# Attention and two-layer FFN on one core: the low part of the weights by an accumulating on-chip transfer, and longer planned TensorE steps for batch 0

## The chip, the cores and the metric

The kernel runs on one core of one Trainium2 chip. The metric is the device time of one execution in microseconds (us), the median of several runs. A profile of one further execution gives the rows that are read below. Engines are named as in the profile: PE (TensorE matrix multiply), PEld (its weight loads), DVE (VectorE), ACT (ScalarE), POOL (GpSimd), SP (SyncE, which issues most transfers).

## What is computed

For each of 8 batches and 8 heads, 576 tokens of 64 numbers: a softmax attention over means of 4 tokens (144 by 144, repeated back to 576) plus a softmax attention over a band of 7 tokens. The sum, 4608 tokens of 512 numbers, goes through a two-layer network:

```
x = attn_out.transpose(0, 2, 1, 3).reshape(B * S, H * D)     # 4608 x 512
h = x @ w_in                                                 # 512 x 2048
g = h * np.cos(h)
return g @ w_out                                             # 2048 x 512
```

The inputs are float32 and the weights arrive as float64. Every product is made of three reduced-precision ones (high by high, high by low, low by high), so each weight, each x and each g is split into a high part, rounded to the matrix format, and a low part, the value minus its high part.

## The kernel before, in words

The network is cut into 12 tiles of 384 tokens and 16 chunks of 128 hidden columns. For each tile and chunk, `gemm1` (L688) makes 12 products of 384 columns, a chain of ACT and DVE steps forms the function (L697 to L706), and `gemm2` (L724) makes 9 products of 512 columns. The first three tiles, which are batches 0 and 1, go through the chunks in groups of four; from tile 3 on each tile takes all 16 chunks at once. Only the first 48 of 192 steps therefore meet a chunk of weights for the first time.

Attention goes by units: a batch and a pair of heads. `u_qk` loads q and k and sums groups of four (L480 on DVE, or L473 and L475 on POOL), `u_v` loads and sums v (L494, L495), `u_s` makes the scores on PE (`l_mm` L518, local; `d_mm` L526, pooled) and the softmax on DVE, ACT and POOL (L537 to L589), `u_t` turns the pooled probabilities (L609) and copies them out (L455, L456), and `u_pv` multiplies with v (L626 pooled, L637 local), adds both (L645) and splits the result into the x tiles (L660 high, L389 low).

Each of the 32 blocks of weights (w_in and w_out, 16 chunks) is loaded by SP (L400) as words and split by `w_split`. ACT takes the absolute value of the upper word into a scratch slot v (L410), DVE builds the float32 value there in four instructions (L411, L413, L415, L417), ACT or DVE writes the high part (L421 or L422), and `sub` writes the low part, v minus high: one tensor_tensor at L389 on POOL, or on DVE where the planner prefers it. v is one of three slots cut from the buffer that later holds the high part of x tile 3.

The order on every engine is that of a planner (`Plan.schedule`). Each step gets an engine, a planned duration, the steps it depends on and sometimes a latency `lat`. The planner runs a list schedule forward and backward eight times, picks an engine where a step has alternatives, and the instructions are issued in the order of the planned starts, so every engine works in order through that list. After planning, a loop puts matmuls on the identity matrix (L841), whose result is never used, into the planned gaps of PE before 300 us. Before each of batch 0's scores, turns and products it puts at least two of them (`warm=2`):

```
n = int((o.start - s[0] - CFG["fgap"]) / (0.43 if ahead or last < 60 else 0.3)) if s else 0
for _ in range(max(n, CFG["warm"] if ahead else 0)):
```

Late partial outputs of tiles 0 to 2 are already written by accumulating transfers that POOL issues (L749, planned at 1.0 us on POOL and a latency of 2.5 us).

Of the kernel before, what the change touches and what calls it, by code (L numbers as in the profile page):

```python
# [12 lines left out]
F32 = mybir.dt.float32  # L13
# [3 lines left out]
AF = mybir.ActivationFunctionType  # L17
ALU = mybir.AluOpType
# [268 lines left out]
def _act(n, psum=True, extra=0):  # L287
    return n * 0.000833 + (0.051 if psum else 0.093) + 0.093 * extra
# [11 lines left out]
def attn_ffn_kernel(ctx: ExitStack, tc: tile.TileContext, qT, kT, vdn, vl, w_in, w_out, out):  # L300
    nc = tc.nc
    pe, act, dve, pool, sp = nc.tensor, nc.scalar, nc.vector, nc.gpsimd, nc.sync
# [6 lines left out]
    pl = Plan()  # L309
# [5 lines left out]
    def psum(tag):  # L315
        pl.banks.append((tag, pl.buf(lambda: ps.tile([P, 512], F32, name="bank", tag=tag, bufs=1), tag)))
        return pl.banks[-1][1]
# [69 lines left out]
    def sub(n, out, in0, in1, **kw):  # L387

        f = lambda e: lambda: e.tensor_tensor(out=out(), in0=in0(), in1=in1(), op=ALU.subtract)  # L389
        pl.op("POOL", _pool(n), f(pool), alts=[("DVE", _dve(n), f(dve))], shares=True, **kw)  # L390
# [11 lines left out]
    def w_split(k, c):  # L402

        pl.name = "w_split"
        wd_b, w = words[(k, c)], wgt[(k, c)]
        wd, n = wd_b.get, DM
        nstage[0] += 1
        v = cut(xx[0], DM * (nstage[0] % 3), [P, DM])
        vi = lambda: v.get().bitcast(I32)
        pl.op("ACT", _act(n, False), lambda: act.activation(v.get(), wd().bitcast(F32)[:, :, 1], AF.Abs), r=[wd_b], w=[v], shares=True)  # L410
        pl.op("DVE", 0.5, lambda: dve.tensor_scalar(out=v.get(), in0=v.get(), scalar1=2.0 ** -15, scalar2=F64_TOP,  # L411
                                                    op0=ALU.max, op1=ALU.min), w=[v], shares=True)
        pl.op("DVE", 0.5, lambda: dve.tensor_scalar(out=vi(), in0=vi(), scalar1=3, scalar2=0x3FFFFFF8,  # L413
                                                            op0=ALU.logical_shift_left, op1=ALU.bitwise_and), w=[v], shares=True)
        pl.op("DVE", 0.7, lambda: dve.scalar_tensor_tensor(out=vi(), in0=wd()[:, :, 1], scalar=-0x40000000, in1=vi(),  # L415
                                                               op0=ALU.bitwise_and, op1=ALU.bitwise_or), r=[wd_b], w=[v], shares=True)
        pl.op("DVE", 0.7, lambda: dve.scalar_tensor_tensor(out=vi(), in0=wd()[:, :, 0], scalar=29, in1=vi(),  # L417
                                                               op0=ALU.logical_shift_right, op1=ALU.bitwise_or), r=[wd_b], w=[v], shares=True)
        h = pl.buf(None)
        hi = lambda: w.get()[:, 0]  # L420
        pl.op("ACT", _act(n, False), lambda: act.activation(hi(), v.get(), AF.Copy), r=[v], w=[h], pw=[w],  # L421
              alts=[("DVE", _dve(n / 2), lambda: dve.tensor_copy(hi(), v.get()))])  # L422
        sub(n, lambda: w.get()[:, 1], v.get, lambda: hi().bitcast(F32), r=[v, h], pw=[w])


    st = {}
# [3 lines left out]
                k=([P, SP_], 1, 1, 0), ptd=([HD, 2, 2, SD], 1, 1, 0),  # L430
# [16 lines left out]
    def bank(b, kind):  # L447

        if b == 0:
            tags = ("pa.0", "po.0", "pa.1", "po.1") if kind == "s" else ("ph.0", "ph.1", "pa.2")  # L450
            return psum(tags[int(pl.turn("early" + str(kind == "s"), len(tags))[-1])])
        return psum(pl.turn("pa", 3))

    def evac(n, dst, src, bk, t, scale=1.0):
        pl.op("ACT", _act(n), lambda: act.activation(dst(), src(), AF.Copy, scale=scale), r=[bk], pw=[t],  # L455
# [44 lines left out]
    def u_s(b, pr):  # L500
        pl.name = "u_s"
        u = st[(b, pr)]
        q, k, qkd = u["q"], u["k"], u["qkd"]
        sml, smd = ub(b, pr, "sml"), ub(b, pr, "smd")
        banks = [bank(b, "s") for _ in range(2)]
        loc, poo = [pl.buf(None) for _ in banks], [pl.buf(None) for _ in banks]

# [4 lines left out]
        def l_mm():  # L512

            for n in range(2 * NSEG):
                for h in range(2):
                    for e in range(2):
                        hs, o, c = slice(64 * h, 64 * h + 64), (8 * (n // 4) + 4 * e + n % 4) * BQ, LQ + BS * (n % NSEG)
                        pe.matmul(banks[n // NSEG].get()[64 * h + BS * e:64 * h + BS * (e + 1), c:c + BS],  # L518
                                  q.get()[hs, o:o + BS], k.get()[hs, o:o + BS], start=True, stop=True)
        pl.op("PE", 0.95, l_mm, r=[q, k], pw=banks, w=loc)  # L520

        def d_mm():
            for i in range(2):
                for h in range(2):
                    hs = slice(64 * h, 64 * h + 64)
                    pe.matmul(banks[h].get()[:HD, i * SD:(i + 1) * SD], qkd.get()[hs, 0, i * HD:(i + 1) * HD], qkd.get()[hs, 1, :],  # L526
                              start=True, stop=True)
        pl.op("PE", 0.65, d_mm, r=[qkd], pw=banks, w=poo)


        mxl, su = sb("mxl", 2, [P, 2 * NSEG]), sb("su", 2, [P, 2 * NSEG + 4])
# [8 lines left out]
        n = 2 * NSEG * BS  # L540
# [7 lines left out]
        for h in range(2):  # L548
# [3 lines left out]
            if not early:  # L552
                using(banks[h], pl.op("DVE", _dve(2 * SD), lambda h=h: dve.tensor_tensor(
                    out=smd.get()[:, h], in0=dq(h), in1=mxd.get()[:, h].unsqueeze(2).broadcast_to([HD, 2, SD]), op=ALU.subtract),
                    r=[poo[h], mx], pw=[smd]))
# [38 lines left out]
    def u_t(b, pr):  # L594
        pl.name = "u_t"
        u = st[(b, pr)]
        sml, smd = u["sml"], u["smd"]
        ptl, ptd = ub(b, pr, "ptl"), ub(b, pr, "ptd")

        pl.op("DVE", _dve(2 * NSEG * BS), lambda: dve.transpose(ptl.get().rearrange("p s q -> p (s q)"),  # L600
                                                                sml.get().rearrange("p s n -> p (s n)")), r=[sml], w=[ptl])
        for h in range(2):
            bk = bank(b, "t")

            def t_mm(h=h, bk=bk):
                for kh in range(2):
                    for qh in range(2):
                        o = kh * SD + qh * HD
                        pe.transpose(bk.get()[:HD, o:o + HD], smd.get()[:, h, qh, kh * HD:(kh + 1) * HD], ident[:HD, :HD])  # L609
            pl.op("PE", 4 * 0.061, t_mm, r=[smd], w=[bk])  # L610
            evac(2 * SD, lambda h=h: ptd.get()[:, h],
                 lambda bk=bk: bk.get()[:HD, :2 * SD].rearrange("p (a n) -> p a n", a=2), bk, ptd)
        u["ptl"], u["ptd"] = ptl, ptd

    def u_pv(b, pr):
        pl.name = "u_pv"
        u = st.pop((b, pr))
        ptl, ptd, vd, vt = (u[n] for n in ("ptl", "ptd", "vd", "vl"))
        xd, xs = ub(b, pr, "xd"), ub(b, pr, "xs")
        banks = [bank(b, "v") for _ in range(2)]  # L620
        poo, loc = pl.buf(None), [pl.buf(None) for _ in banks]

        def d_mm():
            for kh in range(2):
                for h in range(2):
                    pe.matmul(banks[0].get()[64 * h:64 * h + 64, 2 * SD:3 * SD], vd.get()[:, kh, 64 * h:64 * h + 64],  # L626
                              ptd.get()[:, h, kh, :], start=(kh == 0), stop=(kh == 1))
        pl.op("PE", 0.64, d_mm, r=[vd, ptd], pw=[banks[0]], w=[poo])

        def l_mm():  # L630
            for a in range(NSEG // 2):
                for i in range(4):
                    for e in range(2):
                        for h in range(2):
                            r = slice(64 * h + 32 * e, 64 * h + 32 * e + 32)
                            o = (4 * a + i) * BQ
                            pe.matmul(banks[e].get()[64 * h:64 * h + 64, o:o + BQ], vt.get()[r, a, i, :], ptl.get()[r, 4 * a + i, :BQ],  # L637
                                      start=True, stop=True)
        pl.op("PE", 1.52, l_mm, r=[vt, ptl], pw=banks, w=loc)

        evac(SD, xd.get, lambda: banks[0].get()[:, 2 * SD:3 * SD], banks[0], xd, scale=0.25)
        xd.w[-1].deps += poo.w
        half = [pl.buf(None) for _ in range(2)]
        for e in range(2):
            pl.op("DVE", _dve(S // 2), lambda e=e: dve.tensor_tensor(  # L645
                out=xs.get().rearrange("p (a e n r) -> p a e n r", e=2, a=NSEG // 2, r=4)[:, :, e],
                in0=banks[e].get()[:, :12 * BQ].rearrange("p (a n r) -> p a n r", a=NSEG // 2, r=4),
                in1=xd.get().rearrange("p (a e n) -> p a e n", e=2, a=NSEG // 2)[:, :, e].unsqueeze(3).broadcast_to(
                    [P, NSEG // 2, BQ, 4]), op=ALU.add), r=[banks[e], loc[e], xd], pw=[xs], w=[half[e]])
        lo = 0  # L650
        while lo < S:

            tt = tile_of(b * S + lo)
            to = min(S, FROM[tt] + SIZE[tt] - b * S)
            a, m = b * S + lo - FROM[tt], to - lo
            written[tt] += m
            done = pl.buf(None)
            hi = lambda tt=tt, a=a, m=m: x_tile(tt)[0][:, pr, a:a + m]
            src = lambda lo=lo, to=to: xs.get()[:, lo:to]
            pl.op("ACT", _act(m, False), lambda hi=hi, src=src: act.activation(hi(), src(), AF.Copy),  # L660
                  r=[xs], w=[done], pw=[x_b[tt]], alts=[("DVE", _dve(m / 2), lambda hi=hi, src=src: dve.tensor_copy(hi(), src()))])
            sub(m, lambda tt=tt, a=a, m=m: x_tile(tt)[1][:, pr, a:a + m], src, lambda hi=hi: hi().bitcast(F32),
                r=[xs, done], pw=[x_b[tt]])
            lo = to
# [108 lines left out]
    for c in range(NC):  # L773
        for k, d in (("i", 0.0), ("o", 0.7)):
            t = need[c]
# [103 lines left out]
```

## Time and profile before

| | |
|---|---|
| median of 3 runs | 1028.74 us (1027.08 to 1028.91) |
| profiled execution, its own time | 1031.63 us |
| its span, first to last instruction | 1029.5 us |
| busy in the span | PE 97%, PEld 84%, DVE 66%, ACT 59%, POOL 22% |
| mean granted PE clock | 0.983 of full speed |

The span is what the trace covers; the execution's own time has 2.1 us around it. Busy shares are averages over a start, in which attention of the first two batches and the first weights are prepared, and a long stretch of matrix products. The matmuls at L841 count as busy too.

### The profile page before, as it was taken

The numbers are of one execution on the slowest core, as the hardware profiler recorded it, in microseconds if no ns is written. First come the engines' busy times: TensorE is split into PE (matmuls) and PEld (weight loads), VectorE is DVE, ScalarE is ACT, GpSimd is POOL, SyncE is SP. The second block draws the span as 40 slices with busy tenths as digits, with TensorE's granted clock in tenths as the row PEclk, the third lists the DMA queues.
The fourth block names the chain that finished last, engine by engine and source line by source line (L and its number), as shares of the span: only waits on it lengthen the run. The fifth ranks groups of instructions, "written<-read, shape, count | busy, mean of one in ns | idle before, by whom it ended". The sixth has DMA issues, their size and how long they took to land.

```text
span 1029.5 us, 25935 instructions
## 1 busy us (share of the span) xinstructions
PE 1003.0 (97%) x11068; PEld 864.9 (84%) x11068; DVE 676.9 (66%) x1353; ACT 610.6 (59%) x1176; POOL 228.8 (22%) x274
## 2 busy tenths in 40 slices
PE   7889999999999999999999999999999999999998
PEld 4557788889988888889898888888888888899997
DVE  6699889996478668564738856755646865543443
ACT  2546577786566666565646655655655765655554
POOL 5596424433135201010103300101002410000000
PEclk8988899999999999999999999999999999999999
DMA  9762751434245312100202401200101310000000
GB/s 265 237 221 85 242 183 46 61 59 62 32 106 144 76 50 75 59 25 28 76 6 76 133 28 38 96 25 28 55 27 43 120 51 1 32 1 1 31 1 31
DMA packets 36450, 76.11 MB, mean 74 GB/s; under 512 B 3440, under 2 KB 11632, under 8 KB 36336
## 3 DMA queue, kind: packets, MB, share of 16 engines
q1 hardware_dynamic: 32448, 67.38, 20.6%
q0 software_dynamic: 3888, 7.08, 5.0%
q8 instruction: 87, 1.43, 0.6%
q14 instruction: 27, 0.22, 0.1%
HBM read 57.93 MB, written 16.52 MB: 72 GB/s over the span
## 4 chain that ended last, share of the span: by engine, by line
PE 81%; DVE 10%; DMA 4%; ACT 2%; issue 2%; POOL 0%; SPq 0%; ACTq 0%; DVEq 0%; POOLq 0%
PE bank L688 35%; PE bank L724 35%; PE bank L637 3%; PE bank L518 3%; PE bank L526 2%; DMA q<-qT 2%; PE bank L609 2%; DMA wdi<-w_in 1%; PE bank L626 1%; DVE su L577 1%; DVE qkd L480 1%; DVE mxd L550 1%; PE bank L841 1%; DVE gl L389 1%; DVE tr L700 1%
## 5 line engine op out<-in xcount | busy, mean ns | idle before, releaser
L724 PE MATMUL bank<-wo,gh 128*128 128x512 f32 x1152 | 363.3, 396 | 0.0
L724 PEld LDWEIGHTS bank<-wo,gh 128*128 128x128 f32 x1152 | 210.0, 188 | 35.8 <-issue 2.3
L724 PE MATMUL bank<-wo,gl 128*128 128x512 f32 x576 | 228.0, 396 | 0.6 <-POOL su L535 0.6
L699 ACT ACTIVATE tr<-bank,bmagic 128x384 f32<-128x384 f32 x192 | 111.0, 579 | 134.0 <-PE bank L688 122.5
L703 DVE SCALAR_TENSOR_TENSOR tr<-tr,bank 128x384 f32<-128x384 f32 x192 | 105.3, 549 | 121.7 <-ACT tr L698 121.4
L700 DVE SCALAR_TENSOR_TENSOR tr<-tr,bank 128x384 f32<-128x384 f32 x192 | 105.5, 550 | 97.5 <-ACT tr L699 97.3
L697 ACT ACTIVATE tr<-tr 128x384 f32<-128x384 f32 x192 | 100.7, 524 | 84.4 <-DVE tr L700 83.7
L705 ACT ACTIVATE gh<-tr 128x384 fp32r<-128x384 f32 x177 | 92.5, 523 | 90.7 <-DVE tr L703 89.0
L389 DVE TENSOR_TENSOR gl<-tr,gh 128x384 fp32r<-128x384 f32 x160 | 97.3, 609 | 68.6 <-ACT gh L705 67.2
L724 PEld LDWEIGHTS bank<-wo,gl 128*128 128x128 f32 x576 | 108.0, 187 | 24.8 <-POOL su L535 1.0
L688 PE MATMUL bank<-x0h,wi 128*128 128x384 f32 x384 | 109.9, 347 | 0.7 <-DVE tr L703 0.7
L688 PE MATMUL bank<-x1h,wi 128*128 128x384 f32 x384 | 107.6, 341 | 0.0
L688 PE MATMUL bank<-x2h,wi 128*128 128x384 f32 x384 | 107.1, 339 | 0.0
L688 PE MATMUL bank<-x3h,wi 128*128 128x384 f32 x384 | 106.9, 339 | 0.0
L389 POOL TENSOR_TENSOR gl<-tr,gh 128x384 fp32r<-128x384 f32 x32 | 38.1, 1189 | 301.3 <-DVE gh L706 215.8
L698 ACT ACTIVATE tr<-tr 128x384 f32<-128x384 f32 x192 | 100.8, 525 | 6.1
L688 PEld LDWEIGHTS bank<-x0h,wi 128*128 128x128 f32 x384 | 72.1, 193 | 3.7 <-DVE tr L703 0.8
L688 PEld LDWEIGHTS bank<-x1h,wi 128*128 128x128 f32 x384 | 70.7, 189 | 2.9 <-issue 0.8
L688 PEld LDWEIGHTS bank<-x2h,wi 128*128 128x128 f32 x384 | 70.2, 188 | 2.8 <-DVE sml L537 0.6
L688 PEld LDWEIGHTS bank<-x3h,wi 128*128 128x128 f32 x384 | 70.2, 188 | 2.5 <-issue 0.6
L688 PE MATMUL bank<-x0l,wi 128*128 128x384 f32 x192 | 65.8, 342 | 0.0
L688 PE MATMUL bank<-x3l,wi 128*128 128x384 f32 x192 | 64.6, 336 | 0.5 <-POOL x3l L389 0.5
(192 smaller groups left out, 1473.0 us busy)
## 6 DMA issues: line engine op xcount, KB each, us to landing
vl<-vl SPq DMA_DIRECT2D x26, 384.0 KB
out<-ob SPq DMA_DIRECT2D x36, 256.0 KB
wdi<-w_in SPq DMA_DIRECT2D x16, 512.0 KB
wdo<-w_out SPq DMA_DIRECT2D x16, 512.0 KB
q<-qT SPq DMA_DIRECT2D x26, 292.0 KB
k<-kT SPq DMA_DIRECT2D x26, 292.0 KB
vd<-vdn SPq DMA_DIRECT2D x26, 288.0 KB
out<-ob POOLq DMA_DIRECT2D x27, 256.0 KB, 5.7
```

The lines of the kernel that those rows point to most:

```text
L389: f = lambda e: lambda: e.tensor_tensor(out=out(), in0=in0(), in1=in1(), op=ALU.subtract)
L518: pe.matmul(banks[n // NSEG].get()[64 * h + BS * e:64 * h + BS * (e + 1), c:c + BS], q.get()[hs, o:o + BS], k.get()[hs, o:o + BS], start=T ...
L526: pe.matmul(banks[h].get()[:HD, i * SD:(i + 1) * SD], qkd.get()[hs, 0, i * HD:(i + 1) * HD], qkd.get()[hs, 1, :], start=True, stop=True)
L637: pe.matmul(banks[e].get()[64 * h:64 * h + 64, o:o + BQ], vt.get()[r, a, i, :], ptl.get()[r, 4 * a + i, :BQ], start=True, stop=True)
L688: pe.matmul(ph.get()[:, :m], w[:, i, kc, :], x[:, kc, :], start=(n == 0), stop=(n == 3 * KC - 1))
L697: act.activation(tr.get(), tr.get(), AF.Sin, scale=PI)
L698: act.activation(tr.get(), tr.get(), AF.Square)
L699: pl.op("ACT", _act(m, True, 1), lambda: act.activation(tr.get(), h(), AF.Identity, bias=bmagic), r=[ph], w=[tr])
L700: pl.op("DVE", _dve(m), lambda: dve.scalar_tensor_tensor(out=tr.get(), in0=tr.get(), scalar=MAGIC, in1=h(), op0=ALU.subtract, op1=ALU.subt ...
L703: pl.op("DVE", _dve(m), lambda: dve.scalar_tensor_tensor(out=tr.get(), in0=tr.get(), scalar=0.5, in1=h(), op0=ALU.subtract, op1=ALU.mult), ...
L705: pl.op("ACT", _act(m, False), lambda: act.activation(gh.get(), tr.get(), AF.Copy), r=[tr], w=[gh], alts=[("DVE", _dve(m / 2), lambda: dve ...
L724: pe.matmul(o, (gh, gh, gl)[k].get()[:, sl], wo.get()[:, (0, 1, 0)[k]], start=(c == c0 and k == 0), stop=(c == c1 - 1 and k == 2))
```

## The change

The two steps that followed the float32 value v become three: ACT (or DVE) writes the high part, ACT writes minus the high part into the place of the low part, and POOL issues a transfer that adds v to it in place, from on-chip memory to on-chip memory. It is planned as 1.0 us on POOL and 3.0 us of latency. And the PE steps of each unit of batch 0 (five lines of the source, the turn at L609 twice per unit) get a longer planned duration; nothing in the instructions of these steps is changed.

```
-        hi = lambda: w.get()[:, 0]
+        hi, lo = lambda: w.get()[:, 0], lambda: w.get()[:, 1]
         pl.op("ACT", _act(n, False), lambda: act.activation(hi(), v.get(), AF.Copy), r=[v], w=[h], pw=[w],
               alts=[("DVE", _dve(n / 2), lambda: dve.tensor_copy(hi(), v.get()))])
-        sub(n, lambda: w.get()[:, 1], v.get, lambda: hi().bitcast(F32), r=[v, h], pw=[w])
+        pl.op("ACT", _act(n, False), lambda: act.activation(lo(), hi().bitcast(F32), AF.Copy, scale=-1.0), r=[h], pw=[w], w=[v2 := pl.buf(None)])
+        pl.op("POOL", 1.0, lambda: pool.dma_start(lo().bitcast(F32), v.get(), accum_op=ALU.add), r=[v, v2], pw=[w], lat=3.0)
...
+    def slow(b, t, wait=0.0):
+        return t + 0.6 + wait if b == 0 else t
...
-        pl.op("PE", 0.95, l_mm, r=[q, k], pw=banks, w=loc)
+        pl.op("PE", slow(b, 0.95, 0.3), l_mm, r=[q, k], pw=banks, w=loc)
-        pl.op("PE", 0.65, d_mm, r=[qkd], pw=banks, w=poo)
+        pl.op("PE", slow(b, 0.65), d_mm, r=[qkd], pw=banks, w=poo)
-            pl.op("PE", 4 * 0.061, t_mm, r=[smd], w=[bk])
+            pl.op("PE", slow(b, 4 * 0.061), t_mm, r=[smd], w=[bk])
-        pl.op("PE", 0.64, d_mm, r=[vd, ptd], pw=[banks[0]], w=[poo])
+        pl.op("PE", slow(b, 0.64), d_mm, r=[vd, ptd], pw=[banks[0]], w=[poo])
-        pl.op("PE", 1.52, l_mm, r=[vt, ptl], pw=banks, w=loc)
+        pl.op("PE", slow(b, 1.52, 1.2), l_mm, r=[vt, ptl], pw=banks, w=loc)
```

## Rows read from the trace of the kernel before

**Rows 1.** Busy time of each engine in six stretches of the span: the stretch and its length, then busy us (and instructions) of PE, PEld, DVE, ACT and POOL, the granted PE clock, the share of the transfer engines that is busy, and GB/s.

```profile
0.00:20.00 20.00, 13.52 (x387) 7.27 (x391) 14.46 (x33) 5.50 (x21) 13.62 (x36) 0.95 0.93 271
20.00:50.00 30.00, 26.04 (x658) 16.40 (x647) 17.54 (x38) 12.83 (x44) 14.34 (x19) 0.90 0.81 250
50.00:80.00 30.00, 25.89 (x400) 15.45 (x399) 27.97 (x55) 12.45 (x39) 26.67 (x30) 0.78 0.57 190
80.00:115.00 35.00, 30.75 (x601) 23.21 (x599) 31.71 (x61) 22.76 (x58) 18.61 (x18) 0.84 0.45 146
115.00:150.00 35.00, 34.42 (x170) 30.61 (x167) 28.69 (x58) 25.06 (x45) 12.24 (x12) 0.97 0.65 221
150.00:1029.00 879.00, 872.37 (x8882) 771.97 (x8880) 556.54 (x1113) 532.01 (x973) 143.35 (x161) 1.00 0.20 51
```

**Rows 2.** The same view for the instructions of L841 alone (the matmuls on the identity), PE and PEld, in three of these stretches.

```profile
20.00:50.00 30.00, 12.97 (x41) 3.11 (x42) 0.90 0.81 250
50.00:80.00 30.00, 12.04 (x40) 4.10 (x38) 0.78 0.57 190
80.00:115.00 35.00, 5.98 (x21) 1.84 (x21) 0.84 0.45 146
```

**Rows 3.** The chain of work that ended last, in order of time, some pieces from 50 to 105 us: start us, us, what.

```profile
50.40 0.60 DVE xxh L417
...
51.37 0.36 DVE wi L389
...
51.88 0.68 DVE wo L389
...
55.83 0.66 DVE wxi L480
56.49 0.66 DVE wxo L480
57.16 0.84 DVE vd L494
58.02 0.68 DVE vd L495
...
104.27 1.47 POOL wo L389
```

**Rows 4.** The instructions of L389 from 0 to 320 us, those of the weights and one of x tile 3: engine, tiles, count, duration in ns (min/median/max), first and last start in us, shapes.

```profile
L389 DVE TENSOR_TENSOR wi<-xxh,wi x11: 677/680/1039, 51.3 to 231.0; 128x512 fp32r<-128x512 f32 x11
L389 DVE TENSOR_TENSOR wo<-xxh,wo x11: 677/684/1057, 51.9 to 241.4; 128x512 fp32r<-128x512 f32 x11
...
L389 POOL TENSOR_TENSOR wi<-xxh,wi x5: 1257/1483/1823, 78.0 to 206.8; 128x512 fp32r<-128x512 f32 x5
L389 POOL TENSOR_TENSOR wo<-xxh,wo x5: 1299/1482/2553, 101.1 to 190.2; 128x512 fp32r<-128x512 f32 x5
...
L389 DVE TENSOR_TENSOR x3l<-xs,x3h x2: 552/743/934, 242.7 to 299.9; 128x384 fp32r<-128x384 f32 x2
```

**Rows 5.** Timeline of DVE: start us, us, engine, line, operation, tiles and shapes, and in brackets the idle time before it and what ended that.

```profile
28.70 0.31 DVE L456 TENSOR_SCALAR xd<-bank 128x144 f32<-128x144 f32 x1 [4.13 <-PE bank L637]
...
49.94 0.46 DVE L645 TENSOR_TENSOR wxi<-bank,wxi 128x288 f32<-128x288 f32 x1 [5.32 <-ACT wxi L455]
...
86.81 2.78 DVE L583 TENSOR_TENSOR wxo<-wxo,su 72x576 f32<-72x576 f32 x1
...
104.11 0.75 DVE L583 TENSOR_TENSOR wxi<-wxi,su 72x576 f32<-72x576 f32 x1
```

**Rows 6.** Timeline of PE, same columns: blocks of batch 0, one pair of L841, a stop in the middle of a block, and the first products of chunk 1 that need the low part of w_in.

```profile
12.96 1.09 PE L518 MATMUL bank<-wxi,wxo 64*32 64x32 f32 x96
...
14.51 0.71 PE L526 MATMUL bank<-wxo 64*72 64x144 f32 x8
...
37.18 0.42 PE L609 MATMUL bank<-ident,wxo 72*72 72x72 f32 x4
37.43 0.60 PE L841 MATMUL bank<-ident_b 128*128 128x512 bf16 x2
37.96 0.84 PE L626 MATMUL bank<-wxi 72*64 72x144 f32 x8
...
39.26 1.59 PE L637 MATMUL bank<-wxo,wxi 32*64 32x24 f32 x96
...
47.41 0.66 PE L637 MATMUL bank<-wxi,wxo 32*64 32x24 f32 x32 [2.53 <-issue]
...
79.36 1.01 PE L688 MATMUL bank<-x0h,wi 128*128 128x384 f32 x2
```

**Rows 7.** Timeline of POOL, same columns.

```profile
78.03 1.27 POOL L389 TENSOR_TENSOR wi<-xxh,wi 128x512 fp32r<-128x512 f32 x1
...
87.72 1.26 POOL L389 TENSOR_TENSOR wi<-xxh,wi 128x512 fp32r<-128x512 f32 x1
```

**Rows 8.** Timeline of ACT, same columns.

```profile
72.43 0.63 ACT L421 ACTIVATE wi<-xxh 128x512 fp32r<-128x512 f32 x1 [0.33 <-DVE xxh L417]
```

**Rows 9.** The accumulating transfers of before: their issue on POOL (ns, min/median/max), the time from issue to landing of the transfers of that tile, and the queue's packets, MB and share of 16 transfer engines over the span (27 transfers of 256 KB, all of them L749's).

```profile
L749 POOL DMA_DIRECT2D out<-ob x27: 858/911/1219, 178.0 to 338.0; - x27
...
DMA to landing us min/median/max: 3.8/5.7/7.5
```

```profile
q0 software_dynamic: 3888, 7.08, 5.0%
```

## The prediction, made before the changed kernel was run

> **What bounds the kernel now.** I read the table of stretches first. From 150 us on, PE is busy 872.4 of 879 us at full clock, and from 115 to 150 it is busy 34.4 of 35 [rows 1]; nothing that a weight split does to DVE, ACT or POOL there can shorten the end by more than the 7.2 us that these two lines leave. Before 115 us it is otherwise. PE looks full, but the rows of L841 alone show 31.0 of its 82.7 busy us between 20 and 115 to be products that nobody uses [rows 1, 2]. In the same time DVE is busy 28.0 of 30 (50 to 80) and 31.7 of 35 (80 to 115), while ACT has 17.6 and 12.2 us free [rows 1]. The chain of waits says which engine that is: its pieces around 50 to 60 us are mostly DVE's, one instruction behind another [rows 3]. So whatever this change gives or takes, it does before 115 us, and by way of DVE's queue or of the wait for a weight.
>
> **Subtractions removed.** 32 instructions of L389 go: 22 on DVE at 0.68 us and 10 on POOL at 1.48 [rows 4]. Eight of them start before 115.0 us (three on DVE, five on POOL); the others lie beside a PE that is already full, and are worth nothing. Of the three on DVE, two stand on the chain, 0.36 and 0.68 us [rows 3]: **minus 1.0 us**. POOL's five count where DVE waits for them. The plainest place is 86.8 us: a product of 72x576 takes DVE 2.78 us, where the same shape takes 0.75 at 104.1 [rows 5], and it ends just after POOL's subtraction of 87.72 to 88.98 [rows 7]. A DVE instruction with two inputs on chip is held while POOL works. The 1.26 us of that subtraction go: **minus 1.3 us**. (If the place is simply taken by another POOL step: 0. If the whole excess goes: minus 2.0.)
>
> **POOL's one on the chain at 104.27**, 1.47 us of it there [rows 3], holds a scratch slot; ACT's next absolute value waits for it. After the change the slot is held until the transfer lands, later than now. But no block of weights is short at that point, and the planner is told of 4.0 us, so it can put that ACT step behind others: **0**, with ends minus 1.5 (the wait vanishes) and plus 4.7 (below).
>
> **ACT's negatives added.** 32 activations of 128x512 at 0.63 us [rows 8], some eight before 115 us: 5.0 us, against 29.8 us that ACT has free from 50 to 115 [rows 1]. They cost **0** as long as they fall into these gaps; behind them in ACT's queue stand the copies out of PE's banks and the exponentials, and if each of the eight held up one of those by its length, it would be plus 5.0.
>
> **Transfers added.** POOL issues 32 of them. The trace has the same size and kind, though to memory outside: 0.91 us on POOL, 5.7 us to landing, 3.8 to 7.5 [rows 9]. Eight issues before 115 us are 7.3 us of POOL against about 8 taken from it (five at 1.48, the longest 2.55) [rows 4, 9]: even. The moved bytes: 27 transfers took 5.0% of 16 engines' 1029.5 us, 1.9 us each [rows 9]; eight are 15 us in the first 115, where the engines are 45 to 57% busy from 50 on [rows 1]. SP's loads give way a little; none of them is on this part of the chain. The landing matters where PE waits for a low part. That is chunk 1 of w_in: its high part is ready at 73.06 [rows 8], POOL comes to the subtraction only at 78.03 and ends it at 79.30 [rows 7], and PE's first product with the low part starts at 79.36 [rows 6]. Now: 73.06 + 0.63 for the negative + 0.91 for the issue + 5.7 = 80.3, **plus 0.9 us**. Ends: with 3.8, 78.4, no wait; with POOL's queue standing as now, 78.03 + 0.91 + 5.7 = 84.6, plus 5.3. I take the middle because the planner has one step less of POOL's work ahead and knows of the latency.
>
> The Trainium skill (DMA: Bandwidth & Descriptors, section "Anatomy of one DMA — SWDGE (gpsimd) path") fits such a transfer by about 2 us plus its bytes over 436 GB/s, an estimate of 2.6 us for 256 KB. By that the low part would land at 77.2 and the term be 0. The measured 5.7 us of the same size speaks against it, and I keep the row.
>
> **The last split and x tile 3.** The last subtraction starts at 241.4, and the first piece of x tile 3, which takes over the scratch, at 242.7; the next such piece on DVE is at 299.9 [rows 4]. The first will be some 6 us later, and the long distance to the next hides it: **0**; without that cover it would be 6 us of a full PE.
>
> **Batch 0 planned longer.** No instruction of PE is changed; the order is. The new lengths can be held against the rows. A block of L518 takes 1.09 us and the pair of L841 that goes with it 0.60, 1.69 together; planned were 0.95, now 1.85. L526: 0.71 + 0.60 = 1.31; 0.65, now 1.25. L609: 0.42 + 0.60 = 1.02; 0.24, now 0.84. L626: 0.84 + 0.60 = 1.44; 0.64, now 1.24. L637: 1.59 + 0.60 = 2.19; 1.52, now 3.32 [rows 6]. Four are now nearly true, the fifth is 1.1 us too long. The old plan believed PE's results to come 5.1 us per unit earlier (0.9 + 0.6 + two times 0.6 + 0.6 + 1.8), so it put the DVE steps that wait for them too early. The trace shows it: DVE stands 4.13 us at 24.6 and 5.32 us at 44.6 behind a result of PE [rows 5], while right after it come the sums of batch 1 (0.66 + 0.66 + 0.84 + 0.68 = 2.84 us) and 0.60 of a weight split, on the chain [rows 3], all of which depend on nothing of batch 0. A truer plan puts them into the gap of 5.32: **minus 3.4 us**. Ends: both gaps filled, minus 9.45; nothing gained, and L637's four excesses of 1.1 become waiting, plus 4.4. I take the value between because 3.4 us are named steps with rows.
>
> **The sum:** -1.0 - 1.3 + 0 + 0 + 0.9 + 0 - 3.4 = -4.8 us. The profiled execution took 1031.63 us, span 1029.5 and 2.1 around it, 2.9 us above the median of the runs; 1026.8 on its scale is **1024.0** on the median's 1028.74. Its own range is 1019 to 1027.
>
> **Rivals.**
> *The landing takes the place of the subtraction* (slower). Place: POOL's queue and the three scratch slots. For it: POOL is busy 26.7 of 30 us from 50 to 80 [rows 1], so an issue can stand as late as the subtraction did. Price: 5.3 us at chunk 1, and at 104.27 a slot that is free after 0.63 + 0.91 + 5.7 = 7.2 us, not after 2.55 [rows 4], plus 4.7 on ACT's queue. With -2.3 from the subtractions and -3.4 from the plan that is +4.3: 1033.0. It decides once the issue for chunk 1 comes later than 79.36 - 5.7 = 73.7 us. Against it: the planner counts 4.0 us for it. Chance 0.20.
>
> *DVE's relief is eaten by the next wait* (no change). PE stops 2.53 us in the middle of a block at 47.4 for nothing that the trace names [rows 6], and this sets the gap of 5.32, whatever the plan says; granted clock between 50 and 115 is 0.78 to 0.84 [rows 1]. With the plan's 3.4 gone, -1.4: 1027.3. Chance 0.14.
>
> *Both gaps are filled and the slot's wait vanishes* (much faster): -1.0 - 1.3 - 1.5 - 9.45 = -13.2: 1015.5. For it: 31 us of unused products and DVE as the limit [rows 2]. Against: such a plan must be right everywhere. Chance 0.18.
>
> *Issues held up by DVE.* In the trace an issue on POOL took at most 1.22 us, 0.31 over the median, with DVE busy beside it [rows 9]. If each split's issue came behind two DVE instructions with one input and waited 0.4 us for each, eight would be 6.4 us late; half of it on the chain, plus 3.2 to the sum, is 1027.1, no change. Chance 0.05. The Trainium skill (SBUF — State Buffer, section "SBUF: two separate sides", the "DVE blocks DMA" trap) has that rule: while DVE runs a copy in its two-port mode, POOL cannot write the descriptors. The 27 issues here bear out little of it.
>
> **Numbers.** Forecast 0.43, rivals 0.20, 0.14, 0.18 and 0.05. 0.2%, 2.1 us, is about what a measurement of this kernel can tell from no change, so the bounds are 1026.7 and 1030.8. Faster: 0.40 of the first and the 0.18, with 0.03 of the fourth kind and of "no change": 0.61. Same: 0.19. Slower: 0.20. The range takes in the much faster case's and most of the slower one's bounds: 1014 to 1033.
>
> **What would show it.** Right: no L389 of the weights, L645 near 49.9 without a gap of 5 us before it, L480 and L494 of batch 1 ahead of it, PE full some 5 us earlier than 115, and from there the same spacing as now. The landing in the new transfers' rows near 5.7 us. Wrong: ACT's absolute value (L410) or PE's L688 waiting for a transfer for more than 3 us, DVE gaps in batch 0 as long as before, or a stretch behind 150 us in which PE is less busy than now.

## The result, and the profile after the change

The changed kernel takes 1038.46 us (median of 6 runs, 1036.84 to 1041.91) where the kernel before took 1028.83 us beside it (6 runs): a ratio of 1.0078, 95% interval 1.0052 to 1.0104. (The quotient of the two medians is 1.0094; kernels are compared by the ratio below.) It is slower, where 1024.0 and "faster" were forecast, and outside the range. Its profiled execution took 1037.83 us with a span of 1036.1. Line numbers behind L425 are six higher than before (L518 is now L524, L688 is L694, L841 is L847); L410, L421 and L389 kept theirs, L424 is ACT's negative and L425 the issue of the new transfer.

The stretches of the changed kernel, columns as in [rows 1]: length, busy us (and instructions) of PE, PEld, DVE, ACT, POOL, granted PE clock, share of the transfer engines, GB/s.

```profile
20.00:50.00 30.00, 25.52 (x526) 16.09 (x517) 22.02 (x46) 13.59 (x44) 19.75 (x29) 0.73 0.80 239
50.00:80.00 30.00, 25.12 (x491) 16.31 (x489) 25.07 (x50) 15.13 (x44) 19.47 (x21) 0.83 0.79 241
80.00:115.00 35.00, 32.85 (x610) 25.77 (x611) 30.04 (x65) 25.97 (x60) 17.55 (x19) 0.85 0.69 201
115.00:150.00 35.00, 31.23 (x242) 27.89 (x241) 25.51 (x51) 26.09 (x48) 15.40 (x19) 0.90 0.87 249
150.00:1036.00 886.00, 875.83 (x8793) 773.00 (x8792) 547.56 (x1098) 536.39 (x984) 154.75 (x179) 1.00 0.22 55
```

DVE is relieved, though less than the stretch from 50 to 80 says (25.07 instead of 27.97 of 30 us): part of that work moved forward to 20 to 50 (22.02, not 17.54), and from 20 to 150 it is 102.64 us instead of 105.91. The stretch that got worse is the one that the prediction had called full: from 115 to 150 PE is busy 31.23 us, not 34.42. The transfer engines are now busy 0.87 of it instead of 0.65.

How far PE is ahead or behind shows best at single products. Before, then after: the first product of chunk 3 in tile 1 (x1h), of chunk 0 in tile 2 (x2h), and the next chunk (the last line of each; chunks are counted from 0). Columns: start us, us, engine, line, operation, tiles, shapes.

```profile
128.74 0.33 PE L688 MATMUL bank<-x1h,wi 128*128 128x384 f32 x1
...
132.92 0.33 PE L688 MATMUL bank<-x2h,wi 128*128 128x384 f32 x1
...
137.11 0.33 PE L688 MATMUL bank<-x2h,wi 128*128 128x384 f32 x1
```

```profile
124.54 0.33 PE L694 MATMUL bank<-x1h,wi 128*128 128x384 f32 x1
...
129.89 0.62 PE L524 MATMUL bank<-k,q 64*32 64x32 f32 x48
134.23 0.87 PE L524 MATMUL bank<-k,q 64*32 64x32 f32 x48 [3.71 <-ACT ptd L461]
135.03 0.69 PE L694 MATMUL bank<-x2h,wi 128*128 128x384 f32 x1
...
139.01 0.63 PE L730 MATMUL bank<-wo,gh 128*128 128x512 f32 x2
...
141.09 0.33 PE L694 MATMUL bank<-x2h,wi 128*128 128x384 f32 x1
```

At chunk 3 of tile 1 the changed kernel is **4.2 us ahead** (124.54 against 128.74). Two chunks later it is **4.0 us behind** (141.09 against 137.11). Of these 8.2 us, 3.71 are a stop of PE in the middle of an attention block, waiting for ACT. Another 1.9 are the chunk behind it: 135.03 to 139.01 is 3.98 us, where the same products take 2.10 before (128.74 to 130.84). The remaining 2.6 are no full loss: they are blocks of attention and a pair of L847, and the kernel before does the same attention later, from 150.57 to 152.11 us. So the two are best held against each other where PE has done the same products in both, those on the identity aside. That is so at 124.54 and 128.74, and again at chunk 4 of tile 1, before and after:

```profile
169.69 0.44 PE L688 MATMUL bank<-x1h,wi 128*128 128x384 f32 x1
```

```profile
171.32 0.45 PE L694 MATMUL bank<-x1h,wi 128*128 128x384 f32 x1
```

The lead of 4.2 us has become a lag of 1.6: **the place costs 5.8 us**. The granted clock of the stretches shows why that chunk is slow:

```profile
126.00:130.00 4.00, 3.94 (x36) 2.98 (x38) 1.43 (x3) 0.58 (x1) 0.92 (x2) 1.00 1.03 290
130.00:134.00 4.00, 0.52 (x48) 0.40 (x47) 2.02 (x5) 3.12 (x7) 0.00 (x0) 0.77 1.09 331
134.00:139.00 5.00, 4.77 (x60) 4.71 (x61) 3.71 (x8) 2.62 (x6) 0.88 (x1) 0.50 1.05 365
139.00:144.00 5.00, 5.00 (x26) 4.47 (x26) 3.22 (x7) 4.26 (x9) 1.58 (x2) 1.00 0.22 42
```

PE was busy 0.52 of 4 us, and then ran at 0.50, 1.2 GHz, from 134 to 139. What it waited for is read from the chain of waits of the changed kernel (start us, us, what):

```profile
122.39 8.41 DMA wi<-xxh
130.80 0.02 issue
130.82 0.02 ACT xxh L410
130.84 0.54 issue
131.38 0.56 ACT tr L705
131.95 0.42 ACT tr L703
...
132.39 0.52 ACT tr L704
132.91 0.42 ACT tr L703
...
133.36 0.52 ACT tr L704
133.88 0.30 ACT ptd L461
...
134.23 0.87 PE bank L524 x48
135.10 4.07 PE bank L694 x12
```

The new transfer holds its scratch slot for 8.41 us, from its issue to its landing. ACT's next absolute value (L410) needs the slot. ACT works in order, so five steps of the function and the copy at L461, which have nothing to do with weights, stand behind it; PE needs that copy. ACT's timeline shows the stop, and the view of L425 gives all of its kind, first for the two transfers issued between 118 and 126 us and then for all 32:

```profile
130.82 0.66 ACT L410 ACTIVATE xxh<-wdo 128x512 f32<-128x512 f32 x1 [4.22 <-DMA wi<-xxh]
```

```profile
DMA to landing us min/median/max: 6.8/7.6/8.4
```

```profile
  ACT xxh L410: 22.4, 12
...
DMA to landing us min/median/max: 3.3/4.1/8.5
```

ACT stood at L410 12 times for a transfer, 22.4 us together. The planner had been told 1.0 + 3.0 = 4.0 us: true for a quiet transfer (3.3), short for the slow ones.

From 150 us on PE is busy 875.83 of 886 us, 10.2 us idle instead of 6.6 [rows 1]; six of those twelve waits end after 150 us, 0.2 to 2.2 us each. The span is 6.6 us longer (1036.1 against 1029.5). At equal products, 1.6 of them are the lag at chunk 4 of tile 1. Another 2.3 come between chunk 9 of tile 0 and chunk 9 of tile 1 (212.57 to 231.60, where before takes 210.79 to 227.54). There the same wait is at work: ACT stands 2.16 us at L410, L711 is queued right behind it, and PE stops for L711 (the first line is ACT's, the second PE's):

```profile
228.15 0.67 ACT L410 ACTIVATE xxh<-wdi 128x512 f32<-128x512 f32 x1 [2.16 <-DMA wo<-xxh]
```

```profile
229.28 0.73 PE L730 MATMUL bank<-wo,gh 128*128 128x512 f32 x2 [0.73 <-ACT gh L711]
```

That stop explains only 0.73 of the 2.3; the rest are shorter delays whose cause stays open. The last 2.4 come between chunk 12 of tile 2 and chunk 1 of tile 3 (299.41 to 336.57, where before takes 295.39 to 330.17). They are not shown to be the transfer's: the longest stop there, 1.41 us at 307.07 for DVE's L543, comes in e1 below too (1.39 us at 300.75), which has no such transfer.

### The profile page after: what moved, and what is told of

Its sections match the earlier page's. It is cut to its first block, busy times and chain, and to the rows that moved or that the text cites. A ratio compares the mean times of both kernels' runs of the same rounds, so it can differ in the third digit from the quotient of the medians.

```text
span 1036.1 us, 25942 instructions
## 1 busy us (share of the span) xinstructions
PE 1005.8 (97%) x11043; PEld 867.1 (84%) x11043; DVE 665.4 (64%) x1342; ACT 624.0 (60%) x1202; POOL 234.2 (23%) x292
## 3 DMA queue, kind: packets, MB, share of 16 engines
q8 instruction: 86, 1.41, 0.6%
## 4 chain that ended last, share of the span: by engine, by line
PE 80%; DVE 8%; DMA 4%; ACT 3%; POOL 2%; issue 2%; ACTq 0%; SPq 0%; POOLq 0%; DVEq 0%
PE bank L694 33%; PE bank L730 33%; PE bank L643 4%; PE bank L524 3%; PE bank L847 2%; PE bank L532 2%; DMA wi<-xxh 2%; PE bank L615 2%; PE bank L632 1%; DMA wo<-xxh 1%; DMA k<-kT 1%; DVE qkd L486 1%; DVE su L583 1%; DVE tr L706 1%; POOL qkd L481 1%
## 5 line engine op out<-in xcount | busy, mean ns | idle before, releaser
L711 ACT ACTIVATE gh<-tr 128x384 fp32r<-128x384 f32 x171 | 89.3, 523 | 83.0 <-DVE tr L709 81.3
L389 DVE TENSOR_TENSOR gl<-tr,gh 128x384 fp32r<-128x384 f32 x156 | 90.0, 578 | 65.8 <-ACT gh L711 64.4
L694 PE MATMUL bank<-x0h,wi 128*128 128x384 f32 x384 | 109.5, 346 | 2.1 <-DMA wi<-xxh 2.0
L694 PE MATMUL bank<-x2h,wi 128*128 128x384 f32 x384 | 108.6, 343 | 0.8 <-DVE tr L709 0.8
L694 PE MATMUL bank<-x1h,wi 128*128 128x384 f32 x384 | 107.3, 340 | 0.2 <-DVE tr L709 0.2
L694 PE MATMUL bank<-x3h,wi 128*128 128x384 f32 x384 | 106.8, 339 | 0.0
L389 POOL TENSOR_TENSOR gl<-tr,gh 128x384 fp32r<-128x384 f32 x36 | 39.2, 1089 | 294.7 <-DVE gh L712 231.0
L694 PEld LDWEIGHTS bank<-x0h,wi 128*128 128x128 f32 x384 | 71.5, 191 | 6.3 <-DMA wi<-xxh 2.6
L694 PEld LDWEIGHTS bank<-x2h,wi 128*128 128x128 f32 x384 | 71.3, 191 | 3.6 <-DVE tr L709 1.3
L694 PEld LDWEIGHTS bank<-x1h,wi 128*128 128x128 f32 x384 | 70.2, 188 | 3.5 <-DVE tr L709 1.0
L694 PEld LDWEIGHTS bank<-x3h,wi 128*128 128x128 f32 x384 | 70.2, 188 | 2.5 <-issue 0.6
L694 PE MATMUL bank<-x0l,wi 128*128 128x384 f32 x192 | 65.4, 341 | 0.0
L694 PE MATMUL bank<-x2l,wi 128*128 128x384 f32 x192 | 65.2, 340 | 0.0
```

Of the source, the lines that this page charges most:

```text
L694: pe.matmul(ph.get()[:, :m], w[:, i, kc, :], x[:, kc, :], start=(n == 0), stop=(n == 3 * KC - 1))
L711: pl.op("ACT", _act(m, False), lambda: act.activation(gh.get(), tr.get(), AF.Copy), r=[tr], w=[gh], alts=[("DVE", _dve(m / 2), lambda: dve ...
```

## The experiments

Each edit is against the changed kernel. Every variant is planned anew unless it says otherwise, so its order differs everywhere. Ratios are to runs of the kernel before made beside each (medians 1031.78 us for e1 to e4, 1032.01 for e5 to e8, 1032.18 for e9 to e11), and they, not the times, compare kernels. The theory is that **the slot is held longer than planned and ACT stands in front of it**; the rivals are the longer plan of batch 0, the ACT negatives, and weights that come late at PE.

**e1_plan_only.** The old subtraction, with the longer plan kept.
```diff
-        pl.op("ACT", ..., scale=-1.0), ...)
-        pl.op("POOL", 1.0, lambda: pool.dma_start(...), r=[v, v2], pw=[w], lat=3.0)
+        sub(n, lambda: w.get()[:, 1], v.get, lambda: hi().bitcast(F32), r=[v, h], pw=[w])
```


> Only batch 0's TensorE steps planned longer; the low part stays one subtraction on POOL or DVE. Theory L (the transfer's landing is the loss, the longer plan is a gain): faster than before by 3 to 5 us, 1024 to 1026 where before is 1028.8. Rival P (the longer plan is the loss, it delays the first products): 1034 or more. Rival A (ScalarE's extra negatives are the loss): 1024 to 1029, like L.

**e2_transfer_only.** The transfer, with the old plan.
```diff
-        return t + 0.6 + wait if b == 0 else t
+        return t
```


> Only the accumulating transfer with ScalarE's negative; batch 0 planned as before. L: the landing's cost of about 8 us without the plan's gain: 1035 to 1041, no better than the whole change. P: 1027 to 1031, as before. A: 1035 to 1041.

**e3_same_order_pool_sub.** The order of the changed kernel, with a subtraction on POOL where the transfer is issued (planned, untruly, as 1.0 + 3.0).
```diff
-        pl.op("POOL", 1.0, lambda: pool.dma_start(lo().bitcast(F32), v.get(), accum_op=ALU.add), ...
+        pl.op("POOL", 1.0, lambda: pool.tensor_tensor(out=lo(), in0=v.get(), in1=hi().bitcast(F32), op=ALU.subtract), ...
```


> The changed kernel with every engine's order kept; where POOL issues the transfer it subtracts instead (1.3 to 1.8 us), and ScalarE's negative is still written. L: no slot is held for 8 us, so ScalarE's 4.2 us stand at 130 us and TensorE's 3.7 us behind it go, with the 2 us of low clock after them: 1026 to 1031. A: the negatives are all still there, so 1036 to 1040. P: the order is the same, so 1036 to 1040.

Measured: e1 1030.01 us, ratio 0.9988 (0.997 to 1.0005); e2 1044.12, 1.0127 (1.01 to 1.0154); e3 1038.55, 1.0065 (1.0041 to 1.0089). The transfer, with ACT's negative, is the loss, and the longer plan gives some of it back, so that rival falls. By size my expectations missed: e1 came 4 us above the 1024 to 1026 of my theory, e2 3 us above its 1035 to 1041, and e3 in the range that I had given to the rivals. In e2 the wait at L410 is there again, 18.2 us. In e3 it is gone altogether, and PE starts chunk 3 of tile 2 at 140.49 where the changed kernel does so at 149.46; yet e3 ends as late. Its time went elsewhere: from 115 to 150 DVE is busy 34.23 of 35 us and POOL 21.98, and between 150 and 260 PE waits for DVE:

```profile
PE bank L694 <- DVE tr L709: 5.6, 4, 2.0
```

A POOL subtraction of 1.5 us where the plan counts 1.0 is a second wrong price, and it slows DVE besides: the 222 DVE instructions that start from 100 to 250 us in the changed kernel take 130.8 us there and 148.3 in e3, in the same order (one L411 takes 0.42 us there, and 1.52 beside POOL's step of 129.19). As a whole e3 doesn't tell the theory from its rivals; only its first 150 us agree with the theory.

**e4_latency_7.** The transfer told longer. **e5_slot_told** and **e6_weights_told.** The same 4.0 us more, told to the slot alone or to the weight's reader alone, by a step of no engine.
```diff
-..., r=[v, v2], pw=[w], lat=3.0)
+..., r=[v, v2], pw=[w], lat=7.0)                                    # e4
...
+        pl.op("NUL", 0.0, lambda: None, w=[v], lat=4.0)              # e5, behind the transfer
...
+        pl.op("NUL", 0.0, lambda: None, after=[add], pw=[w], lat=4.0) # e6, behind the transfer
```


> The changed kernel with the transfer planned at 7.0 us of latency where it was 3.0 (8.0 with the issue, the slow landings of the trace). L: the planner moves the scratch slot's next user and the first products behind the real landing: 1028 to 1034, better than the change's 1038. A and P: 1036 to 1041, as the change.

> The changed kernel, the transfer still planned at 3.0 us for the products that read the weights, but the scratch slot planned as held 4.0 us longer, by a planner-only step that issues nothing. Theory S (ScalarE's absolute value stands at the slot, and what is queued behind it on ScalarE is late): most of the way to the 1025.3 of the run planned at 7.0, so 1024 to 1031, and L410 waits under 6 us for transfers where it waited 22.4. Rival W (TensorE waits for the low parts themselves): 1035 to 1040.

> The reverse: the products are planned 4.0 us later behind the transfer, the slot's next user is not. S: 1034 to 1041, L410 waits 15 us or more. W: 1024 to 1031.

Measured: e4 1025.30 us, 0.9931 (0.9904 to 0.9958); e5 1028.65, 0.9954 (0.9934 to 0.9975); e6 1035.28, 1.0026 (1.0004 to 1.0049). One number in the plan turns the loss into a gain, with the same steps. Told to the slot it goes with 1.2% (1.0078 to 0.9954), told to the reader with 0.5%, though ACT's waits are then nearly as long as in the changed kernel (20.8 of 22.4 us): a new order moves the time by itself, so 1.2% is no clean price of the slot. Weights that come late at PE are the smaller part: in the changed kernel PE itself waits for one of the new transfers once, 1.97 us, at chunk 1. ACT's waits at L410 for transfers, from 40 to 260 us, follow (us in total, times, longest), e4, e5, e6:

```profile
ACT xxh L410 <- DMA wo<-xxh: 2.4, 2, 2.2
```

```profile
ACT xxh L410 <- DMA wi<-xxh: 0.6, 1, 0.6
```

```profile
ACT xxh L410 <- DMA wo<-xxh: 12.3, 5, 6.0
ACT xxh L410 <- DMA wi<-xxh: 8.5, 7, 2.5
```

In e4 the block that stood 3.71 us runs through in one piece, and at full clock from 115 to 150 us, with PE busy 34.72 of 35:

```profile
130.78 1.02 PE L524 MATMUL bank<-k,q 64*32 64x32 f32 x96
```

```profile
115.00:150.00 35.00, 34.72 (x281) 30.17 (x279) 30.23 (x65) 30.10 (x55) 18.72 (x20) 1.00 0.80 235
```

**e7_negative_only.** The negative is written, then overwritten by the old subtraction. **e8_transfer_told_old_plan.** As e4, with the old plan.
```diff
-        pl.op("POOL", 1.0, lambda: pool.dma_start(...), r=[v, v2], pw=[w], lat=3.0)
+        sub(n, lambda: w.get()[:, 1], v.get, lambda: hi().bitcast(F32), r=[v, h, v2], pw=[w])     # e7
...
-        return t + 0.6 + wait if b == 0 else t
+        return t                                                                  # e8, with lat=7.0
```


> Batch 0 planned longer and ScalarE's negative written, but then overwritten by the old subtraction on POOL or DVE; no transfer. The price of the 32 negatives by themselves, beside the 1030.0 of the run with the longer plan alone. S: 1028 to 1034 (they fall into ScalarE's gaps). Rival A (the negatives' 20 us of ScalarE are part of the loss): 1035 or more.

> The transfer planned at 7.0 us, batch 0 planned as before. If the longer plan is worth about 1 us (as it was alone) and the telling of the latency is what counts: 1024 to 1030. If the gain of 7.0 us needs the longer plan as well: 1032 to 1041.

Measured: e7 1029.51 us, 0.9984 (0.9963 to 1.0005), the same as e1, so 32 more ACT steps cost nothing that can be measured. e8 1036.03, 1.0037 (1.0013 to 1.0061): the wait at L410 is gone there too (0.4 us), and it is still slower than before; PE has stops of another kind in batch 0's blocks (5.5 us at L524 that the trace names as issue, 40 to 150 us). Only both numbers together win. The longer plan is worth 1.1% beside the transfer told at 7.0 (1.0037 to 0.9931), 0.5% beside 3.0, 0.1% beside the subtraction; why it is worth most there stays open. The end of the attention is one place where orders differ: from chunk 12 of tile 2 to chunk 1 of tile 3, with the same products, e1 loses 2.1 us against the kernel before and e5 3.9, while e4 gains 0.3.

**e9_small_loads.** Is the slow landing SP's doing? In the changed kernel SP issues seven loads of weights, 512 KB each, from 121.88 to 126.03, and the transfer issued at 122.39 goes out among them. Queues of the transfer engines in the changed kernel, from 122.4 to 127 and from 127 to 131 us (packets, MB, share of 16 engines; q0 is POOL's queue, q1 SP's):

```profile
q1 hardware_dynamic: 621, 1.14, 97.6%
```

```profile
q1 hardware_dynamic: 419, 0.79, 55.7%
q0 software_dynamic: 206, 0.39, 52.6%
```

For 4.6 us after its issue not one packet of the transfer moves. So in e9 every engine keeps its order and the loads shrink; an eighth of the weights of chunks 6 to 15 is all that is brought, so its output is not the network's.
```diff
+        if c >= 6:                      # chunks 6 to 15
+            dst = lambda: wd.get()[:, :DM // 8]         # and src to match: 64 KB instead of 512 KB
...                                      # w_split reads these 64 words eight times over
```


> The changed kernel, order and plan untouched (transfer told 1.0 + 3.0 us), but SP's loads of the weights of chunks 6 to 15 bring only the first 64 of each 512 words per partition (64 KB instead of 512 KB); the steps of the split read these 64 words eight times over, so the shapes stay and the weights of these chunks are wrong. In the changed kernel the transfer issued at 122.39 us among seven such loads took 8.4 us to land. If that is the backlog of SP's loads: the landings issued from 90 us on fall to 3 to 4 us, ACT's wait at L410 for transfers falls from 22.4 us to under 10, the 3.7 us stop of PE at L524 near 134 us goes, and the time is near 1031 (1028 to 1034). The rival, that the accumulating transfer itself, POOL's issue or DVE beside it is slow: landings of 8 us stay, L410 waits over 15 us, the time is 1036 to 1040. If the load on the transfer engines is not what matters but the first wait at 72 to 79 us (chunks 3 to 6 are loaded there in full in both): no change in the time although the later landings are short.

Measured: 1030.76 us, 0.9974 (0.9953 to 0.9995), within the first expectation. The two transfers issued between 118 and 126 us (121.06 and 126.00; in the changed kernel 122.39 and 125.94, 6.8 to 8.4 us) now land in

```profile
DMA to landing us min/median/max: 3.3/3.9/4.5
```

and PE goes through the same block without a stop and starts tile 2 at 131.01, not 135.03:

```profile
130.03 1.05 PE L534 MATMUL bank<-k,q 64*32 64x32 f32 x96
131.01 0.44 PE L704 MATMUL bank<-x2h,wi 128*128 128x384 f32 x1
```

(Lines are ten higher in e9.) At chunk 4 of tile 1 (166.55), with the same products done, e9 is 3.1 us ahead of the kernel before; it was 4.1 ahead at chunk 3 (124.68). The place costs 0.9 us, not 5.8. That is shown: SP's loads make the landing slow, and the slow landing stops PE. Whether the transfer waits for its turn behind them or for transfer engines that they fill is not told apart. Two expectations missed. The landings issued from 90 us on take 3.3 to 5.7 us, not 3 to 4. ACT's wait at L410 is 13.9 us, not under 10: at 70.92 and 72.42 us e9 still has full loads of chunks up to 5 ahead of its transfers, and ACT waits 4.04 us at 77.63; its other eight waits are of 2.03 us at most. The ratio as a whole also holds whatever else the lighter loads gave; the verdict rests on this block. (The profiled execution of e9 was the slowest of its ten, 1034.19 us, so its end is not compared.)

**e10_latency_5** and **e11_latency_10.** As e4, with 5.0 and 10.0.
```diff
-..., lat=3.0)
+..., lat=5.0)     # e10; lat=10.0 in e11
```


> The changed kernel with the transfer told as 5.0 us of latency instead of 3.0 (7.0 gave 1025.3). Theory that ACT stands at L410 for a slot that the planner believes free too early: the wait at L410 is between 2 and 22 us, about 8, and the time between the two, 1031 (1026 to 1036). Rival, that 7.0 only happened to give a good order: time without relation to the wait, anywhere from 1025 to 1040, with L410's wait unlike the place of the time between the other two.

> The changed kernel with the transfer told as 10.0 us of latency instead of 3.0, longer than any landing measured (8.5). Theory of the slot: no wait at L410 for transfers is left (under 1.5 us in all); the plan gives slots back later than the chip does, which costs little: 1026 (1023 to 1030). Rival, that 7.0 only happened to give a good order: 1030 to 1040 in spite of no wait at L410.

Measured: e10 1025.2 us, 0.9928 (0.9901 to 0.9955); e11 1026.51, 0.9948 (0.9926 to 0.997). So 7.0 was no lucky draw; 5.0, 7.0 and 10.0 agree within their intervals. My expectation of 1031 for 5.0 was wrong, because the sum of ACT's wait is no measure of its cost. e10 waits 11.3 us at L410, and most of it here:

```profile
72.54 0.66 ACT L410 ACTIVATE xxh<-wdi 128x512 f32<-128x512 f32 x1 [6.05 <-DMA wo<-xxh]
```

That lies in the part of the run that has slack: PE stands 6.50 us at L615 about then, and yet e10 starts chunk 3 of tile 0 at 92.56, 6.1 us before the kernel before at the same products, and from 115 to 150 PE is busy 35.00 of 35 us. e4, e10 and e11 beat both kernels.

## Why the prediction was wrong, point by point

**The failed step** is the one headed "POOL's one on the chain at 104.27": "no block of weights is short at that point, and the planner is told of 4.0 us, so it can put that ACT step behind others: 0". I used the planner's figure as if telling it made it so. My own price of the same thing, 5.7 us of landing, was already longer than 4.0, and it had even been taken from the trace [rows 9]. In the same term plus 4.7 stood as the end of the range, and the sum took 0. The place was another (130.82, not 104.27) and so was the victim: not a weight, but ACT's queue behind L410. Measured where the term said 0: 3.71 us of standing and 1.9 at half clock, 5.8 us at equal products, of which e9 with its short landings keeps 0.9. With it fell the end of the first paragraph, "whatever this change gives or takes, it does before 115 us": a PE that is full from 115 to 150 us has nothing to gain there and much to lose.

**The rival** "the landing takes the place of the subtraction" had the mechanism right: scratch slots, and a plus of 4.7 on ACT's queue. It was given 0.20, because "the planner counts 4.0 us for it". The price of +4.3 came from two places, chunk 1 and 104.27, and the largest loss came from a third; there were twelve waits, and the half clock was missing in it.

**Subtractions removed**, -1.0 and -1.3. L389 is gone from the weights and DVE has its time back. But the held product only moved. At 86.31 the 72x576 product takes 0.94 us, not 2.78 [rows 5]; the next one takes 2.25, beside another POOL product that was put there (DVE, then POOL):

```profile
86.31 0.94 DVE L589 TENSOR_TENSOR wxo<-wxo,su 72x576 f32<-72x576 f32 x1
...
100.44 2.25 DVE L589 TENSOR_TENSOR wxi<-wxi,su 72x576 f32<-72x576 f32 x1
```

```profile
100.89 1.17 POOL L589 TENSOR_TENSOR wxi<-wxi,su 128x384 f32<-128x384 f32 x1
```

That is the low end I had named ("the place is simply taken by another POOL step: 0"). The reading behind the term, that such a product "is held while POOL works", was also too simple: the 0.75 us of before at 104.11 [rows 5] has POOL's subtraction of 104.27 [rows 3] beside it, and the 0.94 at 86.31 has a POOL product from 86.71 to 87.84.

**ACT's negatives**: 0, right. They take 0.62 us each, and e7 equals e1.

**Chunk 1's landing**, +0.9: nearly right by luck, out of other numbers. The issue came at 72.42, earlier than reckoned, and the landing took 8.07 us, not 5.7; PE's product waits 1.97 us and starts at 80.53, 1.2 us after 79.36 [rows 6]:

```profile
80.53 0.68 PE L694 MATMUL bank<-x0h,wi 128*128 128x384 f32 x2 [1.97 <-DMA wi<-xxh]
```

The time to landing counts from the start of the issue (122.39 + 8.41 = 130.80), so adding 0.91 for the issue counted it twice: without it the low part lands at 79.4, which makes the term 0. The rival's 7.2 us has the same fault. The fit of the Trainium skill (DMA: Bandwidth & Descriptors, "Anatomy of one DMA — SWDGE (gpsimd) path"), an estimate of 2.6 us, is below every landing here, 3.3 at best and 8.5 at worst.

**x tile 3**: 0, right. Its first piece starts at 248.6, 5.9 us later than before, and PE waits 0.2 us for a piece of that tile, by DVE and not by the transfers.

**Batch 0 planned longer**, -3.4: the mechanism came true, the size did not carry through alone. L645 (now L651) starts at 47.78 with 0.60 us of idle time, not 5.32, and three sums of batch 1 (L486) stand where the gap was; the first gap is still there (4.25 us):

```profile
31.94 0.82 DVE L651 TENSOR_TENSOR xs<-bank,xd 128x288 f32<-128x288 f32 x2 [4.25 <-ACT xd L461]
...
46.44 0.74 DVE L486 TENSOR_REDUCE wxo<-wxi 128x144 f32<-128x576 f32 x1
47.78 0.82 DVE L651 TENSOR_TENSOR wxo<-bank,wxo 128x288 f32<-128x288 f32 x2 [0.60 <-ACT wxo L461]
```

The gain was there, too, and was lost again later. At chunk 3 of tile 1 e1, with this plan and the old subtraction, leads the kernel before by 3.0 us, at chunk 12 of tile 2 still by 2.9, with equal products each time. At chunk 1 of tile 3 only 0.8 are left, and as a whole e1 gains 0.12% (ratio 0.9988, interval 0.997 to 1.0005), about 1.2 us. So the longer plan led by about what was forecast, without setting the end; that the lead came out of this one gap is not shown. The changed kernel was 4.2 us ahead at 124 us, close to the forecast of 4.8; the forecast then took 115 to 150 us as full and therefore safe.

**Issues held up by DVE**: no. The longest of 32 took 1.22 us, the longest of before 1.22 [rows 9]; the Trainium skill's "DVE blocks DMA" trap (SBUF — State Buffer, "SBUF: two separate sides") is not borne out here.

## What to carry to other kernels

Where a planner orders in-order engines, the latency that it is told is part of the kernel. Read the time to landing under the load of the place where the transfer will run, and remember that a buffer read by a transfer stays taken until it lands: here one changed number was worth 1.5%. A wait costs what stands behind it in that engine's queue, so before summing waits, ask which of them lie where the bounding engine has no slack. A full stretch can't be made shorter, but it can be made longer.

## What was not expected of the hardware

A transfer of 256 KB on chip, issued by POOL, lands in 3.3 us at best and took 8.41 among seven loads of 512 KB from SP; the slowest of the run took 8.5, of e4 10.5. For 4.6 us after its issue none of its packets moves, where a quiet one (issued at 157.37, landed after 3.31 us) shows its first after about 1.5. And a stop of 3.71 us cost PE 1.9 us more afterwards, at a granted clock of 0.50 from 134 to 139 us.
